# Two attention and two feed-forward layers on one core: norm statistics, roots and reciprocals move from VectorE to GpSimd, Q is masked for half of the heads only

## The chip, the cores and the metric

The kernel runs on one core of a Trainium2 chip. The metric is the device time in microseconds (us), the median of several runs. Five engines take part. TensorE (PE in the profile, PEld for its weight loads) multiplies matrices. VectorE (DVE) and ScalarE (ACT) work elementwise and can both read PSUM, where the products of TensorE arrive. GpSimd (POOL) works elementwise out of SBUF and issues DMAs. SyncE (SP) issues DMAs.

## The reference

The same attention layer and the same feed-forward layer are applied twice, each behind a norm without gain and bias and each with a residual sum:

```python
B, S, D, H, Dff = 1, 2048, 512, 32, 1792          # Dh = D / H = 16
def _layernorm(x, axis=-1, eps=1e-5):
    m = jnp.mean(x, axis=axis, keepdims=True)
    v = jnp.var(x, axis=axis, keepdims=True)
    return (x - m) / jnp.sqrt(v + eps)
...
q, k, v = qkv[0], qkv[1], qkv[2]
scores = jnp.einsum("bhqd,bhkd->bhqk", q, k) * (Dh ** -0.5)
p = _softmax(scores, axis=-1)
o = jnp.einsum("bhqk,bhkd->bhqd", p, v)
...
x = x + _A_ref(_layernorm(x, axis=-1), A_wqkv, A_wo)
x = x + _B_ref(_layernorm(x, axis=-1), B_w1, B_w2)   # relu(x @ w1) @ w2
x = x + _A_ref(_layernorm(x, axis=-1), A_wqkv, A_wo)
x = x + _B_ref(_layernorm(x, axis=-1), B_w1, B_w2)
```

There are 2 x 32 x 2048 x 2048 exponentials. In blocks of 128 keys by 512 queries that is 4096 blocks.

## The kernel before

The program is straight-line code. While it is written out, a small model of PE's and VectorE's time decides in which order the instructions stand; on the chip each engine then works through its list in order and waits where data is missing. All constants named `..._LAG`, `cost` and `HASTE` belong to that model.

Scores are made in slots of three blocks, in one of two PSUM tiles. ScalarE takes the exponential of two or three of them in one instruction. Where the model finds VectorE free, VectorE takes the third block: its result is the exponential as line, staircase and cube of the mantissa, worked out for two blocks together (a pair).

```python
ex = nc.scalar.activation(out=eb[:, 0 : place[m]], in_=b[:, 0 : place[m]], func=ACTF.Exp,
                          scale=1.0 / (LOG2E * UNIT))                          # L1323
...
first = nc.vector.tensor_scalar(out=lin[...], in0=src, scalar1=EXP_BIAS, ...)   # L1008, per block
nc.vector.tensor_scalar(out=stair, in0=line, ..., op0=ALU.bitwise_and, ...)     # L1049, twice a pair
nc.vector.tensor_mul(out=power, in0=mantissa, in1=mantissa)                     # L1060
nc.vector.tensor_mul(out=power.bitcast(BF16), in0=power, in1=line.bitcast(BF16))# L1064
```

The score matmuls (L1314) contract over 32 rows that hold two heads of 16. Q is therefore written twice, once with the odd head's rows set to zero and once with the even head's:

```python
def q_masked(n, b, w=QS):                                                       # L637
    return nc.vector.tensor_mul(
        out=qbuf[n % 2][:, :, 0:w],
        in0=b.rearrange("p (e q) -> p e q", e=1).to_broadcast((P, 2, w)),
        in1=qmask.rearrange("p (e q) -> p e q", q=1).to_broadcast((P, 2, w)))
```

The sums of the softmax come out of the same matmuls as the values (a column of ones beside V). When a segment (one head, 512 or 256 queries) ends, its PSUM tile is copied to `u`, the sums are brought into shape by a DMA, inverted, brought back by a DMA, and spread over 32 partitions: by a DMA from GpSimd, or by a shuffle on VectorE where it is `quick`. There are three `u` buffers.

```python
nc.vector.tensor_copy(out=u[:, 0:width], in_=ps_o[:, 0:width])                  # L836
nc.sync.dma_start(out=c, in_=sums)                                              # L841
...
quick = sg["load"] is not None or ended[l, j] == NT
def recip():
    nc.vector.reciprocal(out=c, in_=c)                                          # L860
    nc.sync.dma_start(out=sums, in_=c)                                          # L861
    if not quick:
        nc.gpsimd.dma_start(out=r[:, 0:width], in_=...)                         # L863
    mark(("r", n), lag=U_LAG if quick else R_LAG)
def spread_mul():
    if quick:
        spread()                                        # stream_shuffle, L873
    mul(0, width)                                       # scalar_tensor_tensor, L849
```

The norm takes statistics and aggregates on VectorE (L477, L478), a seed of the inverse root by three integer and float instructions (L485 to L492), then three Newton steps: on GpSimd in the middle of the kernel (L510 to L515), on VectorE at its head and tail (L497 to L501).

At the tail, the last 256 rows go through the feed-forward layer alone; W1 streams through four buffers (`load_w1`, L675).

Of the kernel before, what the change touches and what calls it, by code (L numbers as in the profile page):

```python
# [19 lines left out]
EPS = 1e-5  # L20
RSQRT_SEED = 0x5F3759DF
# [3 lines left out]
def kernel(  # L25
# [10 lines left out]
    nc = tc.nc  # L36
# [44 lines left out]
    RSTD_LAG = 5000.0  # L81
# [11 lines left out]
    HASTE = 12  # L93
# [10 lines left out]
    masks = sb([P, 4], FP32, "masks")  # L104
    mask = [masks[:, e : e + 1] for e in range(2)]
    qmask = masks[:, 2:4]
# [49 lines left out]
    stats = [sb([P, nc.vector.BN_STATS_DIM], FP32, f"stats{n}") for n in range(2)]  # L156
# [23 lines left out]
    nc.gpsimd.memset(warm[:], 0.0)  # L180
    nc.vector.memset(ebuf[0][:, 0:QS], 0.0)
# [166 lines left out]
    def rank(t):  # L348
        if "chain" not in t:
            return 2  # L350
        sg = t["chain"]["sg"]
        return 1.5 if sg is segs[seg_at[0]] and sg["left"] <= HASTE else 3

# [119 lines left out]
    def ln_stats(tag, tt, i):  # L473
        if tag not in ln_seq:
            ln_seq.append(tag)
        st = stats[i % 2]
        nc.vector.bn_stats(out=st[:], in_=x_t[tt][:])  # L477
        nc.vector.bn_aggr(out=mv[ln_n(tag)][:, i, :], in_=st[:])  # L478

    def ln_rstd(tag, part):  # L480

        n = ln_n(tag)
        a, y, t1 = va_[n], ya_[n], ta_[n]
        if part == 0:
            nc.vector.tensor_scalar(  # L485
                out=a[:], in0=mv[n][:, :, 1], scalar1=EPS, scalar2=None, op0=ALU.add
            )
            nc.vector.tensor_scalar(
                out=t1[:].bitcast(I32), in0=a[:].bitcast(I32), scalar1=1, scalar2=None,
                op0=ALU.logical_shift_right,  # L490
            )
            nc.vector.tensor_scalar(  # L492
                out=y[:].bitcast(I32), in0=t1[:].bitcast(I32), scalar1=-1.0,
                scalar2=float(RSQRT_SEED), op0=ALU.mult, op1=ALU.add,
            )
            return
        nc.vector.scalar_tensor_tensor(  # L497
            out=t1[:], in0=y[:], scalar=-0.5, in1=y[:], op0=ALU.mult, op1=ALU.mult
        )
        nc.vector.tensor_mul(out=t1[:], in0=t1[:], in1=a[:])  # L500
        nc.vector.scalar_tensor_tensor(  # L501
            out=y[:], in0=t1[:], scalar=1.5, in1=y[:], op0=ALU.add, op1=ALU.mult
        )

    def ln_newton(tag):

        n = ln_n(tag)
        a, y, t1 = va_[n], ya_[n], ta_[n]
        for _ in range(3):
            nc.gpsimd.tensor_mul(out=t1, in0=y, in1=y)  # L510
            nc.gpsimd.tensor_mul(out=t1, in0=t1, in1=a)
            nc.gpsimd.tensor_scalar(
                out=t1, in0=t1, scalar1=-0.5, scalar2=1.5, op0=ALU.mult, op1=ALU.add
            )
            nc.gpsimd.tensor_mul(out=y, in0=y, in1=t1)  # L515
# [20 lines left out]
    def ln_rows(tag, tt, n, i):  # L536

        if tag not in ln_seq:
            ln_seq.append(tag)
        at_tag = ln_seq.index(tag)  # L540
        prev = ln_seq[at_tag - 1]
        rows_of_prev = chunks[prev[1:]][1]
        before_that = ln_seq[at_tag - 2] if at_tag > 1 else None
        old = each(chunks[before_that[1:]][1], "xn", before_that) if at_tag > 1 else []
        if ("st", tag, i) not in made:
            task(830, lambda: ln_stats(tag, tt + i, i), [("st", tag, i)], old)
        if i == n - 1:

            def rstd():
                ln_rstd(tag, 0)  # L550
                ln_newton(tag)
                mark(("rs", tag, 3), lag=RSTD_LAG)

            task(500, rstd, [("rs", tag, 3)], each(n, "st", tag) + old)
            for k in range(n):
                task(
                    325, lambda k=k: ln_apply(tag, tt + k, k), [("xn", tag, k)],
                    [("xT", prev, k)] * (k < rows_of_prev) + [("rs", tag, 3)],
                )
# [76 lines left out]
    def q_masked(n, b, w=QS):  # L636
        return nc.vector.tensor_mul(  # L637
            out=qbuf[n % 2][:, :, 0:w],
            in0=b.rearrange("p (e q) -> p e q", e=1).to_broadcast((P, 2, w)),
            in1=qmask.rearrange("p (e q) -> p e q", q=1).to_broadcast((P, 2, w)),  # L640
        )

    def q_group(n, l, j, T):
        xj, _, w = columns(l, j)
        cost = 90 + 2.09 * w

        def fin(b):
            q_masked(n, b, w)
            mark(("q", n))

        return mm_group(
            q_mms(l, j, T), fin, [("q", n)], each(TPC, "xnT", ("ln1", l, xj)), cost=cost,
            wide_by=w,
        )
# [16 lines left out]
    def load_w1(n):  # L671

        if n < len(chunks) * NF:
            ft = n % NF
            nc.sync.dma_start(  # L675
                out=w1buf[n % NW1][:],
                in_=B_w1[:, ft * P : (ft + 1) * P].rearrange("(c p) f -> p c f", p=P),
            )
            mark(("w1", n), "pe", 4000.0)
# [65 lines left out]

    def rest_of_chunk(l, j):

        b = before(l, j)
        xj, a, w = columns(l, j)
        n = w // P  # L750
        war_h = each(chunks[b][1], "z", *b) if b else []
        work[0:0] = [o_group(l, j, i) for i in range(n)] + ln_groups(
            ("ln2", l, j), xnT[xj], a, n, []
        )
        gs = [h_group(l, j, ft, war_h) for ft in range(0, NF, QS // w)]
        gs += [z_group(l, j, i) for i in range((l, j) == (1, LAST - 1), n)]
        if l == 0:
            gs += ln_groups(("ln1", 1, j), xnT[j], 0, TPC, [])
            gs.append(k_group(1, 0, j))
            gs += [v_group(1, kb) for kb in range(j * TPC, (j + 1) * TPC)]  # L760
            gs += [k_group(1, T, j) for T in range(1, 4)]
        return gs
# [43 lines left out]
    def finish_segment(sg, last):  # L806
# [37 lines left out]
        musts.append((77 + 1.045 * width, now_pe[0] + PE_TO_DVE, copy))  # L844
# [12 lines left out]
        quick = sg["load"] is not None or ended[l, j] == NT  # L857

        def recip():
            nc.vector.reciprocal(out=c, in_=c)  # L860
# [9 lines left out]
            mark(("r", n), lag=U_LAG if quick else R_LAG)  # L870
# [6 lines left out]
        def spread_mul():  # L877
            if quick:
                spread()
            mul(0, width)  # L880

        def direct(i):
            if i == 0:
                spread()
            a = i * P
            nc.vector.reciprocal(out=r[:, a : a + P], in_=r[:, a : a + P])
            mul(a, P)
# [10 lines left out]
        else:  # L898
            task(165, recip, [("r", n)], [("c", n)], place=0)
            cost = 105 + 1.1 * width + (200 + 1.05 * width if quick else 0)  # L900
            task(cost, spread_mul, ots + [("m", n)], [("r", n)] + war)
# [22 lines left out]
    def v_ready(sg, t):  # L924

        found = []
        done = [
            (p, x) for p in pairs if p["sg"] is sg
            for x in p["mms"] if x[4] in made and at([x[4]], "pe") <= t
        ]  # L930
        slots = [s for s in pend if s["ready"] <= t]
        for g in range(4):
# [3 lines left out]
                for s in slots for x in s["blocks"] if x[0] is sg and x[2] == g  # L936
# [42 lines left out]
    def force_v():  # L979
# [6 lines left out]
        if not found:  # L986
            run_until(next(x[4] for p in pairs if p["sg"] is sg for x in p["mms"]))
            found = v_ready(sg, 1e18)
        for home, _, _ in found:
# [95 lines left out]
    idle_matmuls(18)  # L1085
    for e in range(2):
# [5 lines left out]
        nc.vector.tensor_scalar(  # L1092
            out=qmask[:, e : e + 1], in0=mask[e], scalar1=SCALE * LOG2E * UNIT, scalar2=None,
            op0=ALU.mult,
        )
    for i in range(TPC):
        ln_stats(tag, i, i)
    for part in range(4):
        ln_rstd(tag, part)
# [3 lines left out]
    for i in range(TPC):  # L1103
        pt = ln_transpose(tag, i)
        copy = nc.scalar.copy if i % 2 else nc.vector.tensor_copy
        uses(copy(out=xnT[0][:, :, i * P : (i + 1) * P], in_=pt), in_bank[0], "xnT")
        mark(("xnT", tag, i))
        idle_matmuls(1)
    for i in range(3):
# [13 lines left out]
    b = plain(q_mms(0, 0, 0))  # L1123
    uses(q_masked(0, b), in_bank[0])
    mark(("q", 0))
    for kb in range(2):
        b = plain(v_mms(kb))
        uses(nc.scalar.copy(out=v_out(0, kb), in_=v_in(b)), in_bank[0])
        mark(("v", 0, kb))
    work.extend(v_group(0, kb) for kb in range(2, TPC))  # L1130
# [46 lines left out]
    now_pe[0] = 12000.0  # L1177
    now_dve[0] = 13400.0
    exp_end = {-1: 13600.0, 0: 13600.0}
# [5 lines left out]
    while units:  # L1185
# [89 lines left out]
        for sg, kb, g in taken:  # L1275
            sg["left"] -= 1
# [32 lines left out]
        for _ in range(times):  # L1309
            pe_run("s", 1, s_ready)  # L1310
            for a, (sg, kb, g) in sorted(zip(place, now), key=in_turn):
                kt = ktp[sg["l"]][sg["T"]][kb // TPC]
# [3 lines left out]
                    kt[32 * g : 32 * g + 32, kc : kc + P],  # L1316
                    qbuf[sg["n"] % 2][32 * g : 32 * g + 32, sg["e"], 0 : sg["w"]],
# [23 lines left out]
        for sg, kb, g in now:  # L1341
            run_until(("v", sg["l"], kb))
# [47 lines left out]
    for step in range(4):  # L1390
        ln_rstd(tag, step)
# [29 lines left out]
    for ft in range(NF + 1):  # L1421
        if ft < NF:
            n = (l * NQS + j) * NF + ft
            b = more[ft % 4]
            for c in range(NDC):
                add(
                    b, w1buf[n % NW1][:, c, :], xnT[NQS - 1][:, c, at_column : at_column + width],
# [10 lines left out]
            load_w1(n + NW1)  # L1438
# [42 lines left out]
```

## Time and profile before

| what | before |
|---|---|
| median of 3 runs | 1608.02 us (1604.52 to 1611.87) |
| span in the profile | 1606.2 us |
| granted PE clock, mean | 0.992 |
| first exponential starts, last one ends | 16.7 us, 1576.7 us |
| exponentials on ScalarE | 685 of 1536, 680 of 1024, 1 of 512 columns |
| GpSimd busy | 92.9 us |

A line of a group of instructions reads: line of the kernel, engine, operation, what is written and from what, the shapes, how often; then busy time in us and mean nanoseconds of one; then the idle time of the engine just before these instructions and what ended most of it. Successive ScalarE instructions overlap in the records, so the mean of one is more than the time from start to start. A busy PE is not a PE at its peak.

### The profile page before, as it was taken

Reading aid. Unit: us, or ns where it says so; the run is one execution under the profiler, and the core shown is the slowest. Engines: PE = TensorE matmul, PEld = TensorE weight load, DVE = VectorE, ACT = ScalarE, POOL = GpSimd, SP = SyncE. Lnnn points to the kernel's source line nnn. Section 1 sums busy time; section 2 is a strip of 40 time slices with the busy share of each in tenths; the row PEclk is TensorE's granted clock in tenths of the full one; section 3 lists DMA queues with packets and bytes.
Section 4 is the critical chain, followed back from the end, with each engine's and each line's share of the span. In section 5 each row is a group of like instructions: output and inputs, shape, how many; then the busy total and the mean of one; then the engine's idle time right before and its main releaser. Section 6 shows DMA issues by size and latency. Waiting matters only on the chain. (4 is left out here: it accounts for less than half of the span.)

```text
span 1606.2 us, 45384 instructions
## 1 busy us (share of the span) xinstructions
PE 1446.1 (90%) x19833; PEld 541.9 (34%) x19833; DVE 1505.7 (94%) x3012; ACT 1558.0 (97%) x1385; POOL 92.9 (6%) x279
## 2 busy tenths in 40 slices
PE   7988888999999988999889998889989999998997
PEld 3322222322332332232223333223334444544454
DVE  7779999999999999999899999899999999999994
ACT  6999999999999999999999999999999999999994
POOL 2000001000010010100100000001001010010100
PEclk9999999999999999999999999999999999999999
DMA  5000000210001100120001000000210211212031
GB/s 164 2 2 2 2 2 9 47 29 10 9 17 40 28 16 2 27 50 10 15 2 27 21 2 1 2 4 9 54 24 17 42 30 29 59 28 54 14 62 47
DMA packets 113928, 40.61 MB, mean 25 GB/s; under 512 B 103328, under 2 KB 111264, under 8 KB 113728
## 3 DMA queue, kind: packets, MB, share of 16 engines
q1 hardware_dynamic: 101696, 26.21, 7.2%
q0 software_dynamic: 10688, 10.18, 3.6%
q8 instruction: 155, 2.54, 0.7%
q10 hardware_dynamic: 1344, 1.31, 0.2%
q14 instruction: 45, 0.37, 0.1%
HBM read 24.38 MB, written 2.10 MB: 16 GB/s over the span
## 5 line engine op out<-in xcount | busy, mean ns | idle before, releaser
L1323 ACT ACTIVATE e<-ps_s 128x1536 bf16<-128x1536 f32 (+1 forms) x1366 | 1548.1, 1364 | 12.4 <-PE ps_s L1314 7.7
L1314 PE MATMUL ps_s<-q,ktp 32*128 32x512 bf16 (+1 forms) x6192 | 613.6, 341 | 112.2 <-ACT e L1323 97.5
L914 PE MATMUL ps_o<-e,vaug 128*32 128x512 bf16 (+1 forms) x4262 | 501.0, 346 | 16.6 <-DVE u L836 6.8
L1008 DVE TENSOR_SCALAR lin<-ps_s 128x512 int16<-128x512 f32 x680 | 462.3, 684 | 32.9 <-PE ps_s L1314 27.4
L1314 PEld LDWEIGHTS <-ktp 32*128 32x128 bf16 x6192 | 199.9, 91 | 561.5 <-issue 417.5
L914 PEld LDWEIGHTS <-vaug 128*32 128x32 bf16 x6032 | 171.5, 94 | 305.0 <-issue 286.2
L1049 DVE TENSOR_SCALAR step<-lin 128x1024 int16<-128x1024 int16 x680 | 266.2, 417 | 1.1 <-PE ps_o L914 0.4
L1060 DVE TENSOR_TENSOR cube<-step 128x1024 f16<-128x1024 bf16 x340 | 230.2, 680 | 0.9
L1064 DVE TENSOR_TENSOR cube<-cube,lin 128x1024 bf16<-128x1024 f16 x340 | 229.5, 677 | 0.0
L914 PE MATMUL ps_o<-step,vaug 128*32 128x512 bf16 (+1 forms) x858 | 154.3, 341 | 0.0
L442 PE MATMUL ps_f<-xnT,w 128*32 128x512 bf16 (+1 forms) x2016 | 147.4, 345 | 5.7 <-DVE ht L695 3.7
L442 PE MATMUL ps_f<-w,ht 128*32 128x512 bf16 x1624 | 147.1, 381 | 1.6 <-DVE q L637 0.6
L914 PE MATMUL ps_o<-cube,vthird 128*32 128x512 bf16 (+1 forms) x804 | 140.0, 339 | 0.0
L914 PE MATMUL ps_o<-lin,vaug 128*32 128x512 bf16 (+1 forms) x858 | 118.9, 341 | 4.6 <-DVE u L836 3.7
L442 PE MATMUL ps_f<-xnT,wqkv 128*32 128x512 bf16 (+1 forms) x1312 | 106.7, 363 | 3.6 <-DVE vaug L623 1.8
L863 POOL DMA_DIRECT2D r<-u x52 | 36.9, 710 | 1170.2 <-DVE step L1049 383.3
L442 PE MATMUL ps_f<-wo,ot 128*32 128x512 bf16 x960 | 87.1, 381 | 1.5 <-DVE x L661 0.7
L695 DVE TENSOR_SCALAR ht<-ps_f 128x512 bf16<-128x512 f32 x105 | 71.8, 684 | 3.6 <-PE ps_f L442 3.0
L442 PEld LDWEIGHTS <-w 128*32 128x32 bf16 x2016 | 58.4, 96 | 36.0 <-issue 19.2
L637 DVE TENSOR_TENSOR q<-ps_f,masks 128x1024 bf16<-128x1024 f32 (+1 forms) x51 | 53.5, 1049 | 3.5 <-PE ps_s L1314 2.6
L442 PEld LDWEIGHTS <-ht 128*32 128x32 bf16 x1624 | 47.0, 96 | 27.3 <-issue 12.1
L849 DVE SCALAR_TENSOR_TENSOR ot<-u,masks,r 128x512 bf16<-128x512 f32 (+2 forms) x82 | 51.0, 624 | 1.1
(86 smaller groups left out, 653.4 us busy)
## 6 DMA issues: line engine op xcount, KB each, us to landing
w<-in_B_w_dram SPq DMA_DIRECT2D x140, 128.0 KB
r<-u POOLq DMA_DIRECT2D x25, 256.0 KB, 7.3
r<-u POOLq DMA_DIRECT2D x27, 128.0 KB, 4.9
out_dram<-x SPq DMA_DIRECT2D x16, 128.0 KB
x<-in_A_x_dram SPq DMA_DIRECT2D x14, 128.0 KB
w<-in_B_w_dram SPq DMA_DIRECT2D x1, 1792.0 KB
wqkv<-in_A_wqkv_dram ACTq DMA_DIRECT2D x2, 512.0 KB
c<-u SPq DMA_DIRECT2D x48, 8.0 KB
```

Of the source, the lines that this page charges most:

```text
L442: nc.tensor.matmul(out[cols], lhsT[:, cols], rhs, start=i % k == 0, stop=i % k == k - 1, tile_position=(0, 32 * g), skip_group_check=True,)
L637: return nc.vector.tensor_mul(out=qbuf[n % 2][:, :, 0:w], in0=b.rearrange("p (e q) -> p e q", e=1).to_broadcast((P, 2, w)), in1=qmask.rear ...
L695: nc.vector.tensor_scalar(out=out, in0=sums, scalar1=0.0, scalar2=None, op0=ALU.max)
L849: nc.vector.scalar_tensor_tensor(out=ot[t][:, at_column + a : at_column + a + w], in0=u[:, a : a + w], scalar=mask[e], in1=r[:, a : a + w] ...
L863: nc.gpsimd.dma_start(out=r[:, 0:width], in_=bass.AP(tensor=sums.tensor, offset=sums.offset, ap=[list(sums.ap[0]), [0, 32], [1, width]],),)
L914: nc.tensor.matmul(ps_o[32 * g : 32 * g + 32, 0 : sg["w"]], values[:, 4 * sg["T"] + g, 2 * e : 2 * e + 32], rhs, start=g not in sg["begun" ...
L1008: first = nc.vector.tensor_scalar(out=lin[which][:, half * QS : (half + 1) * QS], in0=src, scalar1=EXP_BIAS, scalar2=0.0, op0=ALU.add, op1 ...
L1049: nc.vector.tensor_scalar(out=stair, in0=line, scalar1=keep, scalar2=put, op0=ALU.bitwise_and, op1=ALU.bitwise_or,)
L1060: (609, lambda: nc.vector.tensor_mul(out=power, in0=mantissa, in1=mantissa)),
L1064: (609, lambda: nc.vector.tensor_mul(out=power.bitcast(BF16), in0=power, in1=line.bitcast(BF16))),
L1314: nc.tensor.matmul(b[:, a : a + sg["w"]], kt[32 * g : 32 * g + 32, kc : kc + P], qbuf[sg["n"] % 2][32 * g : 32 * g + 32, sg["e"], 0 : sg[" ...
L1323: ex = nc.scalar.activation(out=eb[:, 0 : place[m]], in_=b[:, 0 : place[m]], func=ACTF.Exp, scale=1.0 / (LOG2E * UNIT),)
```

## The change

Norm: the statistics of a chunk's rows are kept, and GpSimd works out mean and variance from them and the inverse root as a power of -0.5, in nine small instructions. At head and tail VectorE keeps aggregates and root, with a seed in fewer instructions and two steps instead of three. Reciprocals of the softmax sums become a power of -1 on GpSimd. Q is written unmasked for the even heads, and the masked half for the odd heads is made from it in SBUF; the even heads' score matmuls contract over 16 rows. Fewer spreads are shuffles. At the head the first scores stand behind one V projection instead of two. At the tail W1 lies ready in buffers that are free by then, and the last segment is read out of PSUM without a copy. The aim is to take small work off VectorE and to shorten head and tail.

```diff
-    RSTD_LAG = 5000.0
+    RSTD_LAG = 4000.0
-    HASTE = 12
+    HASTE = 8
...
-        nc.vector.bn_stats(out=st[:], in_=x_t[tt][:])
-        nc.vector.bn_aggr(out=mv[ln_n(tag)][:, i, :], in_=st[:])
+        nc.vector.bn_stats(out=stats[ln_n(tag)][:, i, :], in_=x_t[tt][:])
...
+            pool = nc.gpsimd
+            pool.tensor_tensor(out=t1, in0=st[:, :, 1], in1=st[:, :, 4], op=ALU.subtract)
+            pool.tensor_mul(out=t1, in0=t1, in1=t1)
...
+            pool.tensor_tensor(out=ya_[n][:, 0:rows], in0=a, in1=masks[:, 4:5].to_broadcast((P, rows)), op=ALU.pow)
...
-    def q_masked(n, b, w=QS):
-        return nc.vector.tensor_mul(
...
+    def q_raw(n, b, w=QS):
+        return nc.vector.tensor_scalar(
+            out=qbuf[n % 2][:, 0, 0:w], in0=b, scalar1=SCALE * LOG2E * UNIT, scalar2=None,
+            op0=ALU.mult,
+        )
+    def q_odd(n, w=QS):
+        nc.vector.tensor_scalar(
+            out=qbuf[n % 2][:, 1, 0:w], in0=qbuf[n % 2][:, 0, 0:w], scalar1=mask[1],
+            scalar2=None, op0=ALU.mult,
+        )
...
+        if (l, j) == (1, LAST - 2):
+            for ft in range(NF):
+                home = (w1buf[...] if ft < NW1 else (kt01 + kt2)[(ft - NW1) // 2]...)
+                w1_last.append(home)
+                if ft >= NW1:
+                    nc.sync.dma_start(out=home, in_=B_w1[:, ft * P : (ft + 1) * P]...)
...
-        quick = sg["load"] is not None or ended[l, j] == NT
+        quick = ended[l, j] == NT or sg["load"] is not None and ended[l, j] >= NT - 2
         def recip():
-            nc.vector.reciprocal(out=c, in_=c)
+            nc.gpsimd.tensor_tensor(
+                out=c, in0=c, in1=masks[:, 5:6].to_broadcast((P, width // 32)), op=ALU.pow
+            )
             nc.sync.dma_start(out=sums, in_=c)
...
-            mark(("r", n), lag=U_LAG if quick else R_LAG)
+            mark(("r", n), lag=500.0 + (U_LAG if quick else R_LAG))
...
         def direct(i):
+            source = ps_o if last else u
...
-    b = plain(q_mms(0, 0, 0))
-    uses(q_masked(0, b), in_bank[0])
+    q_bank = plain(q_mms(0, 0, 0))
+    uses(q_raw(0, q_bank), at_q)
+    q_odd(0)
-    for kb in range(2):
-        b = plain(v_mms(kb))
-        uses(nc.scalar.copy(out=v_out(0, kb), in_=v_in(b)), in_bank[0])
+    b = plain(v_mms(0))
+    uses(nc.vector.tensor_copy(out=v_out(0, 0), in_=v_in(b)), in_bank[0])
...
+                rows = slice(32 * g, 32 * g + 16 * (1 + sg["e"]))
-                    kt[32 * g : 32 * g + 32, kc : kc + P],
-                    qbuf[sg["n"] % 2][32 * g : 32 * g + 32, sg["e"], 0 : sg["w"]],
+                    kt[rows, kc : kc + P],
+                    qbuf[sg["n"] % 2][rows, sg["e"], 0 : sg["w"]],
...
-        for sg, kb, g in now:
-            run_until(("v", sg["l"], kb))
```

The last lines move where a V projection is forced: no longer when a slot's scores are issued, but when its values are multiplied. Since the model decides the order, every one of these edits also shifts the places of the instructions around it.

## The prediction

> **What bounds the kernel now.** I read the busy shares on the page first, then the chain, then the groups with shapes kept apart.
>
> ```profile
> PE 1446.1 (90%) x19833; PEld 541.9 (34%) x19833; DVE 1505.7 (94%) x3012; ACT 1558.0 (97%) x1385; POOL 92.9 (6%) x279
> ACT 7%; PE 5%; DVE 3%; issue 1%; DMA 0%; ACTq 0%; DVEq 0%
> L1323 ACT ACTIVATE e<-ps_s 128x1536 bf16<-128x1536 f32 (+1 forms) x1366 | 1548.1, 1364 | 12.4 <-PE ps_s L1314 7.7
> ```
>
> ScalarE (ACT) is busy 97% of 1606.2 us, nearly all in the exponentials. Between the first and the last of them it stands idle only 12.4 us. So the kernel is a head, a row of 1366 exponentials, and a tail. The chain is no proof of this: it was followed back for only a part of the span, and TensorE (PE) and VectorE (DVE) in it are close behind ScalarE.
>
> ```profile
> L1323 ACT ACTIVATE e<-ps_s 128x1536 bf16<-128x1536 f32 x685 | 1026.9, 1574 | 8.2 <-PE ps_s L1314 4.2 <-PE ps_o L914 3.6
> L1323 ACT ACTIVATE e<-ps_s 128x1024 bf16<-128x1024 f32 x680 | 733.1, 1153 | 4.2 <-PE ps_s L1314 3.5 <-PE ps_o L914 0.4
> L1008 DVE TENSOR_SCALAR lin<-ps_s 128x512 int16<-128x512 f32 x680 | 462.3, 684 | 32.9 <-PE ps_s L1314 27.4
> L1049 DVE TENSOR_SCALAR step<-lin 128x1024 int16<-128x1024 int16 x680 | 266.2, 417 | 1.1 <-PE ps_o L914 0.4
> L1060 DVE TENSOR_TENSOR cube<-step 128x1024 f16<-128x1024 bf16 x340 | 230.2, 680 | 0.9
> L1064 DVE TENSOR_TENSOR cube<-cube,lin 128x1024 bf16<-128x1024 f16 x340 | 229.5, 677 | 0.0
> ```
>
> The two sizes show the exchange that the kernel lives by. A slot has three blocks of 512 scores; in 680 slots VectorE takes one of them with its own approximation, and ScalarE's instruction is 1024 wide. The starts of successive ScalarE instructions lie 1331 and 904 ns apart in the trace (medians), so one block moved saves ScalarE 427 ns. A pair of blocks costs VectorE 2 x 684 + 2 x 417 + 680 + 677 = 3559 ns. VectorE time is therefore worth something only where the schedule turns it into pairs.
>
> ```profile
> L637 DVE TENSOR_TENSOR q<-ps_f,masks 128x1024 bf16<-128x1024 f32 x35 | 42.6, 1217 | 2.4 <-PE ps_s L1314 1.7 <-PE ps_f L442 0.4
> L873 DVE STREAM_SHUFFLE r<-u 128x512 f32<-128x512 f32 x23 | 16.7, 727 | 0.0
> L510 POOL TENSOR_TENSOR ta<-ya 128x4 f32<-128x4 f32 x48 | 14.3, 298 | 286.3 <-DVE ya L492 283.8
> L478 DVE BATCH_NORM_AGGREGATE mv<-stats 128x2 f32<-128x6 f32 x64 | 11.7, 182 | 2.2
> L860 DVE RECIPROCAL c<-c 128x16 f32<-128x16 f32 x48 | 11.6, 242 | 0.0
> ```
>
> These are what the change takes from VectorE. Last, the one stretch where ScalarE starves, by windows of 3 us:
>
> ```profile
> 153.00:156.00 3.00, 2.13 (x20) 0.66 (x24) 2.09 (x5) 1.46 (x2) 0.00 (x0) 0.74 0.02 5
> 156.00:159.00 3.00, 3.00 (x24) 0.61 (x19) 1.84 (x5) 1.66 (x2) 0.00 (x0) 0.50 0.02 3
> 159.00:162.00 3.00, 3.00 (x24) 0.68 (x21) 2.53 (x6) 2.26 (x2) 0.00 (x0) 0.50 0.00 0
> 162.00:165.00 3.00, 3.00 (x26) 0.58 (x23) 1.96 (x4) 1.84 (x2) 0.00 (x0) 0.55 0.03 3
> ```
>
> After the durations come busy PE, PEld, DVE, ACT, POOL, then the granted PE clock. ScalarE works 7.23 of 12 us because the clock is halved: 4.8 us of its idle time in one place. The timeline just before shows PE waiting for a VectorE that does a shuffle and a product back to back. Two shorter clock halvings, at 270 and 393 us, cost about 0.9 us each.
>
> **What the Trainium skill says.** "VectorE: DVE Perf Modes", section on the perf-mode tier table: a tensor_scalar on bf16 in SBUF reaches four elements a cycle, PSUM sources in fp32 only one. The trace agrees: 1024 elements from PSUM take 1217 ns, 1024 int16 in SBUF 417. "SBUF — State Buffer", section "SBUF: two separate sides": GpSimd and a VectorE instruction in a two-port mode lock each other out for a whole instruction. The trace agrees weakly: the step instruction (median 417 ns) reaches 571 ns, and those that overlap a GpSimd instruction average 428 against 416 ns. "GPSIMD Engine Reference", section "Performance versus the Vector engine", prices an add but no power; no row here has one. "TensorE: Matmul & The Clock Gate", Part 1: the clock falls to half after an idle window of about 3.4 us. The trace agrees with half (0.50), in pieces of 3.4, 6.8 and 10.2 us.
>
> **The change part by part.** Counts come from the instruction lists of the two programs.
>
> VectorE loses: 58 aggregates x 182 = 10.6 us; 16 three-instruction seeds x (162 + 170 + 170) = 8.0; the 78 reciprocals, 11.6 + 5.7 (30 of 128x8) = 17.3; 11 shuffles x 727 = 8.0, which become GpSimd DMAs. Q: 36 x 1217 becomes 36 x (684 for a 128x512 PSUM read, as row lin, + about 285 for a bf16 SBUF product; I choose the four-per-cycle price, between 296 for the 544-wide scaling of V and half of 417), 8.9 us less; the 16 narrow ones about 0.7. Head and tail roots, masks and the last copy about 1.8 less, two V copies taken over from ScalarE 1.4 more. Together 54 us off. It gains 9 pairs (340 to 349) x 3559 = 32.0. So VectorE should be busy about 1506 - 54 + 32 = 1484 us. Most of what is freed does not come back as pairs; it becomes slack, and slack on an engine that is not the last one is worth nothing directly.
>
> ScalarE keeps 1366 exponentials, but 18 change from 1536 to 1024: 18 x 427 ns = **7.7 us off**, all on the path.
>
> Head: the first exponential starts at 16.7 us. Three small root instructions fewer (0.2 us each from start to start) and copies of the transposes shared better give about 0.6 us. Q's first half is ready after 684 instead of 1225 ns, 0.5 us, and scores for the even heads need nothing else of it. The first scores no longer stand behind the second V projection and twelve matmuls of other work: in the trace Q ends at 15.15 and scores start at 16.31, so 1.0 of that gap can go. **2.1 us off**; first exponential at about 14.6.
>
> Tail, 29.5 us from the last exponential (1576.7): the copy out of PSUM goes (0.42, 0.47 with its gap), three root instructions of 0.2 (0.6), and the wait for streamed W1 at 1599.0 (0.55 beyond the 0.87 us rhythm of the loop). **1.6 us off**. The chain puts 3.33 us on that DMA, but most of it ran beside matmuls that would take the time anyway.
>
> Interior idle, 12.4 us: the shuffle that stood before the clock halving is now a DMA, so I expect some of the 4.8 us to go, but halvings may come elsewhere, as 58 fewer score matmuls (the spare repeats that keep PE busy) are issued. I take **2.5 off**, choosing half.
>
> GpSimd: 192 Newton instructions become 16 x 9 = 144, of which 16 are powers of 128x4; 78 powers of 128x16 or 128x8 are added. I don't know the price of a power. The reciprocal, 242 ns on VectorE, now starts when its DMA lands instead of when VectorE comes to it. In the trace a spread by DMA has landed about 14.1 us after the copy of the sums (512 wide), and its product starts 15 to 16 us after: about 1 us of slack; 256 wide about 3.5. A power under 1 us is hidden. Sixteen-row contraction for even heads changes no matmul's columns: zero.
>
> Sum: 7.7 + 2.1 + 1.6 + 2.5 = 13.9 us off 1608.0: **1594 us**, 0.9% faster.
>
> **Rivals.** (1) The power is slow, 2 us or more. For it: it is another kind of function than the multiplies at 252 to 298 ns, and it can lock out the step instructions, one every 2.3 us. Against it: the schedule's allowance for the root falls from 5000 to 4000 ns, and the reciprocal gets 500. At 2 us, some 25 products would make VectorE wait 1 us each, and 78 locks, each met by a step instruction with chance 2/2.3 and outlasting it by 1 us on average, cost 68 us more (an estimate from these rows): 93 us, against 1606 - 1484 = 122 us of idle time. Most is absorbed, but ScalarE starves in places: 1605 to 1625. (2) Moved spreads collide with the three u buffers. At 1026 to 1071 us, where keys end early, three copies span about 17 us, and a DMA spread plus product takes 15 to 16: a wait of 1 to 3 us for up to eleven spreads, with clock halvings after it. 1600 to 1610. (3) VectorE was the true limit and 22 us of net relief come through everywhere. Against it, ScalarE's interior idle is 12.4 us; even all of it gone gives 1584.
>
> **Range and chances.** Steps one to three are counts times measured durations, some 11.4 us with 2 us of doubt. Idle time can fall by 9 or rise by 12, and the three times of before lie 7 us apart. So 1585 to 1606 holds eight in ten. 2% is 32 us; ScalarE's blocks forbid that gain, and only a slow power gives that loss.
>
> **What would show it.** Exponentials of 1024: 698, busy ScalarE near 1540 in that line, first one near 14.6 us; VectorE near 1484; tail near 28 us; reciprocal row on GpSimd under 1 us; product rows waiting no longer than now (1.1 us in all); no halving near 155 us. I am wrong if a power takes over 1.5 us, if ScalarE's idle time between exponentials exceeds 20 us, or if the clock is halved over more than the 20.5 us of now.

## The result, and the profile after

The changed kernel takes 1648.24 us (median of 4, 1645.15 to 1654.62), the kernel before 1607.34 in the same comparison: ratio 1.0257, 95% interval 1.0218 to 1.0296. It is slower by 2.6%, where 0.9% faster was predicted.

The page of the changed kernel, first the busy shares, then the granted PE clock in 40 slices, then two groups:

```profile
PE 1511.5 (92%) x19838; PEld 540.1 (33%) x19838; DVE 1493.4 (91%) x2905; ACT 1560.2 (95%) x1383; POOL 314.9 (19%) x322
...
PEclk9999878679999999899899999877999999999999
...
L1373 ACT ACTIVATE e<-ps_s 128x1536 bf16<-128x1536 f32 (+1 forms) x1366 | 1551.5, 1335 | 55.4 <-PE ps_s L1364 52.9
...
L893 POOL TENSOR_TENSOR c<-c,masks 128x16 f32<-128x16 f32 (+1 forms) x78 | 210.6, 2700 | 875.8 <-DMA c<-u 856.9
```

ScalarE now waits 55.4 us before its exponentials instead of 12.4, nearly all for the score matmuls. VectorE is less busy than before, and TensorE is busier, though it runs 58 score matmuls fewer: it works at a lower clock. The same row of the page of the kernel before has no slice under 9:

```profile
PEclk9999999999999999999999999999999999999999
```

In the clock record of the trace the stretches at half clock (halvings) add up to 199 us, of which 5 us lie at the very end, where PE runs out of work; before they were 27, of which 7 lie in the tail. The profile thus divides the 40.7 us by which the span grew: the first exponential starts at 14.7 instead of 16.7 us (-2.1), the tail is 27.3 instead of 29.5 us (-2.2), and the stretch between first and last exponential is 1604.9 instead of 1560.0 us (+45.0).

The worst stretch, in the first attention layer, by windows (busy PE, PEld, DVE, ACT, POOL, then PE clock, DMA share, GB/s):

```profile
260.00:275.00 15.00, 13.24 (x160) 3.99 (x152) 14.79 (x29) 15.00 (x15) 3.68 (x2) 1.00 0.11 19
275.00:290.00 15.00, 14.59 (x101) 3.16 (x99) 10.96 (x23) 11.61 (x11) 6.09 (x10) 0.52 0.01 2
290.00:305.00 15.00, 15.00 (x108) 3.61 (x105) 10.69 (x23) 10.97 (x9) 0.79 (x1) 0.50 0.14 27
305.00:317.00 12.00, 12.00 (x95) 2.56 (x92) 7.33 (x13) 8.49 (x8) 0.00 (x0) 0.52 0.10 23
317.00:332.00 15.00, 13.41 (x171) 4.48 (x165) 15.00 (x30) 15.00 (x14) 3.73 (x2) 1.00 0.23 47
```

From 276 to 317 us the clock stays at half. PE is busy all the time, while VectorE and ScalarE stand idle for a quarter of it or more: they wait for PE, not PE for them. What PE ran in that stretch, shapes kept apart:

```profile
L1364 PE MATMUL ps_s<-q,ktp 16*128 16x512 bf16 x70 | 15.9, 608 | 0.0
L1364 PE MATMUL ps_s<-q,ktp 32*128 32x512 bf16 x17 | 6.9, 608 | 0.4 <-ACT e L1373 0.4
```

and in the 26 us after it, when the clock was full again:

```profile
L1364 PE MATMUL ps_s<-q,ktp 32*128 32x512 bf16 x62 | 8.5, 381 | 0.6 <-ACT e L1373 0.4
L1364 PE MATMUL ps_s<-q,ktp 16*128 16x512 bf16 x19 | 4.1, 382 | 0.9 <-ACT e L1373 0.9
```

A matmul over 16 rows lasts as long as one over 32 (382 and 381 ns at full clock, 608 at half). But the slow stretch belongs to the even heads, 70 of 87 score matmuls with 16 rows; the fast one to the odd heads, 19 of 81. Over the whole kernel up to 1140 us this is a lean and no more: of the score matmuls that start at half clock 314 of 495 have 16 rows (63%), of those at full clock 1506 of 3030 (50%).

No idle spell of PE stands ahead of these halvings. The 3.4 us just before two of them, the first of which is the one at 276 us:

```profile
272.30:275.70 3.40, 2.39 (x26) 0.89 (x24) 3.40 (x8) 3.40 (x4) 0.00 (x0) 1.00 0.00 0
200.60:204.00 3.40, 2.69 (x27) 0.74 (x24) 3.32 (x8) 3.40 (x5) 0.00 (x0) 1.00 0.00 0
```

Ahead of all halvings of the changed kernel but the one at the very end, PE is busy 2.2 to 2.8 of 3.4 us, and its longest gap there is 0.95 us. The idle window of about 3.4 us that the prediction spoke of does not precede these halvings.

Nor does it fall everywhere. Late in the kernel it stays full:

```profile
1200.00:1400.00 200.00, 184.83 (x3380) 83.15 (x3383) 195.62 (x392) 199.45 (x178) 60.77 (x49) 1.00 0.16 31
1400.00:1600.00 200.00, 185.51 (x3954) 96.36 (x3958) 195.45 (x392) 198.36 (x180) 47.35 (x50) 1.00 0.25 52
```

From 1140 to 1640 us, 1258 of 2609 score matmuls have 16 rows too; most of the 2609 are 256 columns wide instead of 512. Why the clock holds there was not tested.

The step of the prediction that said "zero" for the sixteen rows is the one to test.

### The profile page after: what moved, and what is told of

It reads as the page before. It is cut to its first block, busy times and chain, and to the rows that moved or that the text cites. A ratio compares the mean times of both kernels' runs of the same rounds, so it can differ in the third digit from the quotient of the medians.

```text
span 1646.9 us, 45349 instructions
## 1 busy us (share of the span) xinstructions
PE 1511.5 (92%) x19838; PEld 540.1 (33%) x19838; DVE 1493.4 (91%) x2905; ACT 1560.2 (95%) x1383; POOL 314.9 (19%) x322
## 4 chain that ended last, share of the span: by engine, by line
ACT 61%; PE 21%; DVE 13%; DMA 3%; issue 2%; POOL 0%; ACTq 0%; DVEq 0%
ACT e L1373 60%; PE ps_s L1364 8%; PE ps_o L954 7%; PE ps_f L444 4%; DVE lin L1061 4%; DVE step L1102 2%; DVE cube L1113 2%; DMA r<-u 1%; DVE cube L1117 1%; PE ps_s L1425 1%; DVE ht L709 1%; DVE ot L882 1%; DMA w<-in_B_w_dram 1%; DMA wqkv<-in_A_wqkv_dram 1%; PE ps_f L534 0%
## 5 line engine op out<-in xcount | busy, mean ns | idle before, releaser
L1373 ACT ACTIVATE e<-ps_s 128x1536 bf16<-128x1536 f32 (+1 forms) x1366 | 1551.5, 1335 | 55.4 <-PE ps_s L1364 52.9
L1364 PE MATMUL ps_s<-q,ktp 32*128 32x512 bf16 (+3 forms) x6134 | 638.1, 358 | 88.0 <-ACT e L1373 76.2
L954 PE MATMUL ps_o<-e,vaug 128*32 128x512 bf16 (+1 forms) x4240 | 521.6, 360 | 13.5 <-DVE u L866 6.9
L1061 DVE TENSOR_SCALAR lin<-ps_s 128x512 int16<-128x512 f32 x698 | 474.1, 683 | 49.6 <-PE ps_s L1364 45.4
L1364 PEld LDWEIGHTS <-ktp 32*128 32x128 bf16 (+1 forms) x6134 | 195.0, 93 | 570.1 <-issue 407.9
L893 POOL TENSOR_TENSOR c<-c,masks 128x16 f32<-128x16 f32 (+1 forms) x78 | 210.6, 2700 | 875.8 <-DMA c<-u 856.9
L444 PE MATMUL ps_f<-xnT,w 128*32 128x512 bf16 (+1 forms) x2016 | 157.8, 362 | 6.3 <-DVE ht L709 2.8
L954 PE MATMUL ps_o<-cube,vthird 128*32 128x512 bf16 (+1 forms) x830 | 148.6, 351 | 0.2 <-DVE cube L1117 0.2
L954 PE MATMUL ps_o<-lin,vaug 128*32 128x512 bf16 (+1 forms) x880 | 132.0, 362 | 6.1 <-DVE u L866 3.8
L898 POOL DMA_DIRECT2D r<-u x63 | 48.5, 770 | 162.2 <-DVE step L1102 49.0
L882 DVE SCALAR_TENSOR_TENSOR ot<-u,masks,r 128x512 bf16<-128x512 f32 (+1 forms) x78 | 49.9, 640 | 4.2 <-DMA r<-u 4.2
```

The lines of the kernel that those rows point to most:

```text
L444: nc.tensor.matmul(out[cols], lhsT[:, cols], rhs, start=i % k == 0, stop=i % k == k - 1, tile_position=(0, 32 * g), skip_group_check=True,)
L882: nc.vector.scalar_tensor_tensor(out=ot[t][:, at_column + a : at_column + a + w], in0=u[:, a : a + w], scalar=mask[e], in1=r[:, a : a + w] ...
L893: nc.gpsimd.tensor_tensor(out=c, in0=c, in1=masks[:, 5:6].to_broadcast((P, width // 32)), op=ALU.pow)
L898: nc.gpsimd.dma_start(out=r[:, 0:width], in_=bass.AP(tensor=sums.tensor, offset=sums.offset, ap=[list(sums.ap[0]), [0, 32], [1, width]],),)
L954: nc.tensor.matmul(ps_o[32 * g : 32 * g + 32, 0 : sg["w"]], values[:, 4 * sg["T"] + g, 2 * e : 2 * e + 32], rhs, start=g not in sg["begun" ...
L1061: first = nc.vector.tensor_scalar(out=lin[which][:, half * QS : (half + 1) * QS], in0=src, scalar1=EXP_BIAS, scalar2=0.0, op0=ALU.add, op1 ...
```

## The experiments

Three theories. **Rows**: matmuls over 16 rows count less toward keeping the clock up than those over 32, so the clock falls while even heads are worked on. **Slow power**, rival (1) of the prediction: powers of 3 us hold up the products, PE starves, the clock falls after it. **Schedule**: the model placed things worse, or the 58 spare repeats fewer leave PE too idle. (Spare repeats are score matmuls issued again only to keep PE busy; the last one counts.)

| run | edit | median us | ratio, 95% interval | PE clock |
|---|---|---|---|---|
| after | the change | 1648.24 | 1.0257 (1.0218 to 1.0296) | 0.940 |
| e1_rows32 | after, 32 rows, even Q unmasked | 1598.61 | 0.9934 (0.9918 to 0.9950) | 0.993 |
| e2_before_rows16 | before, 16 rows for even heads | 1662.48 | 1.0326 (1.0304 to 1.0348) | 0.931 |
| e3_recip_dve | after, reciprocals on VectorE | 1657.08 | 1.0291 (1.0269 to 1.0314) | 0.931 |
| e4_q_masked | after, Q's part undone | 1607.20 | 0.9990 (0.9978 to 1.0002) | 0.989 |
| e5_q_gpsimd | after, 32 rows, even Q masked by GpSimd | 1631.86 | 1.0139 (1.0114 to 1.0165) | 0.976 |
| e6_before_rows24 | before, 24 rows for even heads | 1629.87 | 1.0127 (1.0086 to 1.0168) | 0.974 |
| e7_repeats32 | after, spare repeats over 32 rows | 1622.00 | 1.0074 (1.0051 to 1.0096) | 0.969 |
| e8_more_repeats | after, three times the repeats | 1657.21 | 1.0275 (1.0246 to 1.0304) | 0.98 |
| e9_q_masked_recip_dve | e4, reciprocals on VectorE | 1607.19 | 0.9991 (0.9981 to 1.0001) | 0.995 |
| e10_q_zero_dma | after, 32 rows, even Q zeroed by DMA | 1632.58 | 1.0143 (1.0118 to 1.0168) | 0.974 |
| e11_q_masked_cheap | e4, lower price in the model | 1604.18 | 0.9971 (0.9957 to 0.9986) | 0.990 |

The ratios are to the kernel before, run beside each on the same chip. The clock is the mean of the profiled execution; for e8 it is that of four timed executions (0.972 to 0.982), as the profiled one was disturbed and is not read.

**e1: rows alone, in the changed kernel.** The instruction lists of PE and VectorE stay exactly as they were. Left out is the mask of the even heads' Q: their scores take in the odd head's product, so the numbers are others, the work is the same.

```diff
-                rows = slice(32 * g, 32 * g + 16 * (1 + sg["e"]))
+                rows = slice(32 * g, 32 * g + 32)
```

> The changed kernel with the score matmuls of the even heads contracting over all 32 rows again; Q stays unmasked, so the even heads' scores take in the odd head's product, and every engine's list of instructions stays as it is. Rows theory (matmuls over 16 rows count less toward keeping PE's clock up): the halved clock goes from about 194 us back to 40 us or less, mean clock 0.98 or more, time 1593 to 1602 us, ratio to before about 0.994. Slow-power theory (GpSimd powers of 2.7 us hold up products and starve PE): time stays near 1645, clock 0.94. Schedule theory (fewer spare repeats and other places of instructions starve PE): also near 1645.

Measured: 1598.61 us and clock 0.993; the halvings add up to 25 us. Busy shares and clock of its page:

```profile
PE 1442.7 (90%) x19834; PEld 537.0 (34%) x19838; DVE 1490.0 (93%) x2905; ACT 1550.0 (97%) x1383; POOL 316.7 (20%) x322
...
PEclk9999999998999999999999999989999999999999
```

PE is busy 69 us less than in the changed kernel with the same list of matmuls. The powers on GpSimd are all there. Slow power and schedule both said about 1645 and fall as causes of the loss.

**e2: rows alone, in the kernel before.** Q is masked there, so 16 rows give the same scores:

```diff
+                rows = slice(32 * g, 32 * g + 16 * (1 + sg["e"]))
-                    kt[32 * g : 32 * g + 32, kc : kc + P],
-                    qbuf[sg["n"] % 2][32 * g : 32 * g + 32, sg["e"], 0 : sg["w"]],
+                    kt[rows, kc : kc + P],
+                    qbuf[sg["n"] % 2][rows, sg["e"], 0 : sg["w"]],
```

> The kernel before with one edit: even heads' score matmuls contract over 16 rows. Q is masked there, so the scores are the same. Rows theory: clock falls to about 0.94, halved for some 150 to 220 us, time 1640 to 1660 us. Slow-power theory and schedule theory: no change, 1607 us, clock 0.99.

Measured: 1662.48 us, a little above the expected range, with the clock at 0.931 and halved for 232 us. Score matmuls and clock in its profile, first by form:

```profile
L1315 PE MATMUL ps_s<-q,ktp 16*128 16x512 bf16 x1912 | 345.6, 423 | 36.8 <-ACT e L1324 32.1 <-DVE lin L1008 1.2 <-DVE stats L477 0.3
L1315 PE MATMUL ps_s<-q,ktp 32*128 32x512 bf16 x1934 | 337.4, 412 | 36.1 <-ACT e L1324 30.2 <-DVE lin L1008 1.9 <-DVE ot L849 0.2
```

then the clock on its page:

```profile
PEclk9998768999999999999797999858999999999889
```

The dips lie near those of the changed kernel, around 150 to 260, 790 to 880 and 1070 to 1140 us. Both forms got slower than the 384 ns of the kernel before, because both run at the lowered clock. The rows that were left out had held zeros in Q; so it is not the values of Q that count, but that the rows take part. The edit alone costs 53 us here, and its undoing in the changed kernel earns 50 (1648.24 to 1598.61). With nothing else changed, the rows alone make the loss, in both kernels. A matmul and its weight load lose the rows together, and no run separates the two.

**e3: the slow powers.** One line: VectorE's reciprocal in the same place.

```diff
-            nc.gpsimd.tensor_tensor(
-                out=c, in0=c, in1=masks[:, 5:6].to_broadcast((P, width // 32)), op=ALU.pow
-            )
+            nc.vector.reciprocal(out=c, in_=c)
```

> The changed kernel with the reciprocals of the softmax sums on VectorE again, in the same places of the list, all else changed. Rows theory: still slow, 1635 to 1650 us, clock 0.94 to 0.95. Slow-power theory: 1593 to 1605 us, clock 0.98 or more. Schedule theory: near 1645.

Measured: 1657.08, 7 us beyond the range of the rows theory and far from the 1593 to 1605 of the slow power. The interval of its ratio overlaps that of the changed kernel, so nothing is won or lost for certain.

**e4: Q's part undone as a whole.**

```diff
-        return nc.vector.tensor_scalar(
-            out=qbuf[n % 2][:, 0, 0:w], in0=b, scalar1=SCALE * LOG2E * UNIT, ...)
+        return nc.vector.tensor_mul(
+            out=qbuf[n % 2][:, :, 0:w], in0=b...to_broadcast((P, 2, w)),
+            in1=qmask...to_broadcast((P, 2, w)))
```

> The changed kernel with Q's part undone as a whole: both halves masked by one product of 1217 ns, 32 rows for all heads; norm, reciprocals, spreads, head and tail as changed. VectorE has about 9 us more work than in the changed kernel. Rows theory: 1594 to 1604 us, clock 0.98 or more, ratio about 0.995. Slow-power theory: near 1645, as the powers are still there. Schedule theory: anything, as the model's list changes.

Measured: 1607.20, clock 0.989. The clock is back as the rows theory says, but the time misses its range by 3 us: it is 8.6 us above e1. The model, which prices the product at 1160 ns and the two small instructions at 821, placed 688 blocks on VectorE instead of 698 (10 x 427 ns = 4.3 us); the first exponential starts 0.9 us later than in e1; most of the rest is idle time (16.4 instead of 12.7 us between exponentials).

**e6, e7, e8: how it grades.** Twenty-four rows in the kernel before (`24 + 8 * sg["e"]` in place of `16 * (1 + sg["e"])`):

> The kernel before with even heads contracting over 24 rows (8 of them masked to zero, so the scores are the same). Rows theory, graded: between 32 and 16 rows, so halved for 50 to 150 us and 1615 to 1645 us. Rows theory with a threshold: like one of the two, about 1609 or about 1660. If it is something in the 16-row form itself and not the number of rows: about 1609.

Measured: 1629.87, clock 0.974, halved for 87 us: 21 us for 8 rows left out, against 53 for 16. The loss grades with the rows over these three points, and it is no property of the 16-row form alone.

In the changed kernel, 32 rows for the spare repeats alone, which change no result:

```diff
+                rows = slice(32 * g, 32 * g + (32 if turn + 1 < times else 16 * (1 + sg["e"])))
```

> The changed kernel, except that the spare repeats of a score matmul (some 1000 of 6134, overwritten by the last one) contract over 32 rows for the even heads too; only the last, the one that counts, has 16 rows there. About 500 of 3078 matmuls change. Rows theory: the halved clock falls in part, to 80 to 170 us, time 1620 to 1640 us. Schedule or slow-power theory: as the changed kernel, 1645 to 1655.

Measured: 1622.00 (15 executions, 1609.61 to 1631.36), halved for 102 us in the profiled one. Some 500 matmuls of 3078 take back about half of the loss, and the wide scatter suggests that the clock is then near the point where it falls.

More repeats for all heads, the even heads' over 16 rows:

```diff
-    FLOOR = 0.56
+    FLOOR = 0.8
```

> The changed kernel with the model's floor for PE's load raised from 0.56 to 0.8: 8313 score matmuls instead of 6134, all added ones being spare repeats; even heads keep 16 rows. If what holds the clock up is the share of time in which PE runs anything at all, the halvings go nearly away and the time is 1598 to 1615 us. If it is rows times time, they go in part: 1615 to 1640 us. If repeats delay what matters: over 1645.

Measured: 1657.21. The clock rises to about 0.98, yet the time doesn't fall. Of the 2179 added repeats 1160 are over 16 rows and 1019, those of the odd heads, over 32, so this run doesn't tell whether work over 16 rows by itself holds the clock up. That the repeats stand ahead of the matmuls that ScalarE waits for, and so cost what the clock earns, is argued from the list, not shown by a profile.

**e5 and e10: mending Q at VectorE's lower price.** GpSimd masks the even half in place, or four DMAs of SyncE zero its rows:

```diff
+            nc.gpsimd.tensor_scalar(                                       # e5
+                out=qbuf[n % 2][:, 0, 0:w], in0=qbuf[n % 2][:, 0, 0:w], scalar1=mask[0], ...)
...
+            for g in range(4):                                             # e10
+                rows = slice(32 * g + 16, 32 * g + 32)
+                nc.sync.dma_start(out=qbuf[n % 2][rows, 0, 0:w],
+                                  in_=qbuf[n % 2][32 * g : 32 * g + 16, 1, 0:w])
```

> The changed kernel with 32 rows for all heads and right scores at VectorE's lower price: Q is written unmasked, VectorE makes the odd half from it as in the change, and GpSimd then masks the even half in place (the first Q is masked by VectorE, straight from PSUM). Rows theory: the clock is back (0.98 or more) and the rest of the change earns what it earned with 32 rows and unmasked Q: 1597 to 1606 us, ratio 0.992 to 0.997. If instead VectorE loses the freed time to GpSimd's locks, with 52 more GpSimd instructions, 1606 to 1615.

> The changed kernel with 32 rows for all heads, where the odd heads' rows of the even half of Q are set to zero by four small DMAs from SyncE (copied from rows of the odd half that are zero already; the first Q is masked by VectorE out of PSUM). VectorE's work is that of the changed kernel. Rows theory: as with unmasked Q and 32 rows, 1597 to 1604 us, ratio about 0.994, clock 0.985 or more. If SyncE's queue, which waits in order for sums and W1, brings the zeros late: PE waits for Q as it did behind GpSimd's queue, and 1610 to 1635 us.

Measured: 1631.86 and 1632.58, both far above e1. Score matmuls run over 32 rows in both. The waits in the two, e5 over the whole span, by waiting group:

```profile
L1378 PE MATMUL ps_s<-q,ktp 32*128 32x512 bf16 (+1 forms) x6134 | 618.3, 346 | 112.8 <-ACT e L1387 84.1 <-POOL q L660 14.6 <-DVE lin L1066 5.6
L660 POOL TENSOR_SCALAR q<-q,masks 128x512 bf16<-128x512 bf16 (+1 forms) x51 | 82.5, 1617 | 499.4 <-DVE q L649 355.3 <-PE ps_s L1378 126.3 <-PE ps_o L959 10.1
```

and e10 from 1000 to 1110 us, by releaser (us in total, times, longest):

```profile
ACT e L1386 <- PE ps_s L1377: 24.6, 17, 7.7
...
PE ps_s L1377 <- DMA q<-q: 17.1, 4, 7.1
```

Where the passes over the keys are short, near 1000 to 1200 us, Q is asked for soon after it is made, and the mask stands in an in-order queue behind powers and spreads (e5), or behind sums and W1 (e10). PE's waits for Q themselves are 15 and 25 us, and more than half of the halved time (72 us in e5 between 480 and 1212 us, 78 in e10 between 384 and 1214) begins in such an idle spell of PE or just after it. How much of the 33 us each makes was not taken apart.

**e9 and e11: what the other parts are worth at full clock.** e9 is e4 with VectorE's reciprocal and the model's prices of before for it.

> The changed kernel with Q masked by one product and 32 rows for all heads (the 1607 us run), and the reciprocals on VectorE again, with the model's prices and allowances of before. It tells what the slow powers (about 3.2 us for 128x16) are worth where the clock is not the trouble. If they hold products up: 1598 to 1605 us. If they are hidden and VectorE's 17 us were worth having: 1609 to 1616 us. If both are hidden: within 3 us of the other.

Measured: 1607.19 against 1607.20. Where the clock is not the trouble, no difference shows between the 78 reciprocals on GpSimd and on VectorE. e11 sets the model's price of Q's product lower:

```diff
-        cost = 90 + 2.09 * w
+        cost = 760 * w / 512
```

> Q masked by one product and 32 rows, as in the 1607 us run, but the model's price of that product is set to 760 ns (it takes 1217), so that it places 700 blocks on VectorE instead of 688. If the 10 blocks fewer were what that run lost against the one with unmasked Q (1598.6 us): 1599 to 1604. If VectorE can't carry them beside the dearer product: 1606 to 1615.

Measured: 1604.18 us, ratio 0.9971 (0.9957 to 0.9986), with 700 blocks on VectorE:

```profile
L1378 ACT ACTIVATE e<-ps_s 128x1536 bf16<-128x1536 f32 x665 | 996.0, 1558 | 9.4 <-PE ps_s L1369 8.2 <-PE ps_o L956 0.7
L1378 ACT ACTIVATE e<-ps_s 128x1024 bf16<-128x1024 f32 x700 | 745.5, 1135 | 8.1 <-PE ps_s L1369 7.7
```

It is the one kernel here with the reference's work in full that beats both: by 0.3% the kernel before, by 44 us the changed one.

## Why the prediction was wrong

The step that failed is the sentence "Sixteen-row contraction for even heads changes no matmul's columns: zero." The duration of a matmul is indeed unchanged, 382 against 381 ns. But the clock that all matmuls share fell, and with it the supply of scores: about 50 us. The prediction had the clock in view, as a small term of interior idle time with "halvings may come elsewhere", and named 58 fewer repeats as the danger; it looked at how long PE is busy, not at how many of its rows are. All three of its signs of being wrong came; the first of them, a power of over 1.5 us, had no part in the loss.

The Trainium skill, "TensorE: Matmul & The Clock Gate", Part 1, describes a monitor of how busy PE has been. Busy time in the profile does not tell this clock: PE was busy 15.00 of 15 us from 290 to 305 us with the clock at 0.50, and in the kernel before, where all score matmuls have 32 rows, 3.00 of 3 us from 159 to 162 us at 0.50. That the rows in use enter is what e1, e2 and e6 show; the page doesn't speak of them.

With rows restored (e1), the other steps can be read:

- **Blocks moved to VectorE.** 698 exponentials of 1024, as counted; 7.7 us predicted, 6.0 us shorter from first to last exponential, with idle time 0.8 us up (12.7 against 11.9). Right within 1 us.
- **Head** 2.1 predicted; 2.1 in the changed kernel, 2.6 in e1. **Tail** 1.6; 2.2 and 2.5. Both right in direction, the tail mis-sized by 0.6 to 0.9: the halving of 3.4 us at 1588 us in the kernel before comes back in neither e1 nor the changed kernel, which may be the difference.
- **Interior idle** 2.5 off predicted; in e1 nothing was gained. The halving near 155 us did go, and all of its 4.8 us with it. But the one near 390 us grew from 6.8 to 10.2 us, and 5.2 us of idle time came between 1050 and 1100 us. Wrong: the sum counted nothing for rival 2, below.
- **Sum**: e1 is 10.7 us under the kernel before, against 11.4 for the first three steps and 13.9 for all.
- **VectorE** 1484 us busy predicted, 1493 measured. The odd half of Q takes 350 ns, not 285, and for 256 columns the two small instructions (413 + 287) save nothing over 683.
- **Rival 1, a slow power.** Slow it is:

```profile
L893 POOL TENSOR_TENSOR c<-c,masks 128x16 f32<-128x16 f32 x48 | 151.9, 3165 | 683.7 <-DMA c<-u 683.5
L893 POOL TENSOR_TENSOR c<-c,masks 128x8 f32<-128x8 f32 x30 | 58.7, 1956 | 192.2 <-DMA c<-u 173.4 <-issue 18.8
```

At two to three times the price that I called hidden, nothing is lost by it (e9). GpSimd starts it 1.9 us after the copy of the sums, when the DMA lands, where VectorE came to its reciprocal after 3.5 us or more; so the spread of 512 columns lands 15.0 us after the copy (median) instead of 14.1, and VectorE waits for spreads 4.2 us in the whole run. The estimate of 68 us for locks was wrong as well: 180 step instructions that overlap GpSimd average 424 ns against 417, and the 87 of them that start inside a power with more than 0.6 us left to run average 419. A lock that lasts for a whole power does not show.

- **Rival 2, the moved spreads.** It came true in one place, and it is most of what went wrong with interior idle time. In e1, near 1030 to 1060 us, spreads by DMA land 6.5 to 8.5 us apart. One product starts 19.6 us after its copy, just as its spread lands at 1054.4 us (start in us, length, instruction, idle time before it and what ended it):

```profile
1054.44 0.75 DVE L882 SCALAR_TENSOR_TENSOR ot<-u,masks,r 128x512 bf16<-128x512 f32 x1 [3.38 <-DMA r<-u]
1056.45 0.39 PE L1364 MATMUL ps_s<-q,ktp 32*128 32x512 bf16 x3 [2.87 <-DVE lin L1061]
1056.89 1.45 ACT L1373 ACTIVATE e<-ps_s 128x1536 bf16<-128x1536 f32 x1 [2.68 <-PE ps_s L1364]
```

VectorE waits for the spread, PE for VectorE, ScalarE for PE, and from 1056.9 us the clock is halved for 10.2 us. In the kernel before, where these spreads are shuffles, ScalarE loses 0.1 us there. e9, with the reciprocals on VectorE, has the same wait (4.2 us) and a halving of 10.2 us from 1054.6 us, so it is not the power that makes it. In the changed kernel two such products come 19.1 to 19.4 us after their copies, at 1098.7 and 1105.4 us. No run put the shuffles back.

## What to carry to other kernels

A contraction over fewer rows was free in the instruction's duration here (382 against 381 ns) and not free in the clock (0.992 to 0.931 in the kernel before): before rows that hold zeros are dropped from matmuls in a kernel whose clock is halved now and then, count what is left in rows, not only in time. When an engine shows more busy time for fewer instructions, read the granted clock first and compare one shape in two stretches. A slow instruction in a helper's queue cost nothing where its result was due late (the powers, e9); the same queue cost PE 15 us where it also served something due soon (the mask of Q, e5).

## What was not expected of the hardware

Clock against rows, in one kernel with nothing else changed: 32 rows for all heads, clock 0.992, 1607 us; 24 rows for the even heads, 0.974, 1630 us; 16 rows for them, 0.931, 1662 us. Rows that held zeros in Q kept the clock up like others: 0.992 in the kernel before, with the zeros, 0.993 in e1, without them.

A power on GpSimd takes 864 ns for 128x2, 1108 for 128x4, 1956 for 128x8 and 3165 for 128x16, 0.12 to 0.21 us for each further element of a partition, where the other operations on 128x4 beside it take 0.2 to 0.35 us in all. A mask of 128x512 in bf16 takes GpSimd 1.8 us (e5).
